# Attention with a GpSimd side job: another timetable for the side job, subtractions a slot earlier, one small transfer on another queue, two exponentials at another place

## The chip, the core and the metric

The program runs on one core of one Trainium2 chip. A core has TensorE (PE, matrix products into PSUM banks of 128 x 512 float32; its weight loads are shown apart as PEld), VectorE (DVE), ScalarE (ACT), GpSimd (POOL) and SyncE (SP). SP computes nothing here: it issues DMA transfers, and ACT can issue them too. Each engine works through its own list of instructions in order; an instruction that waits holds up all that stands behind it on that engine. The metric is the device time of one execution in microseconds (us).

## The reference

A transformer block of sequence length S = 2048 and width D = 448, cut to what matters here:

```python
h = layernorm(x) * (1 + ca) + sa                       # ca, sa, ... from silu(c) @ w_mod
q, k, v = split(h @ wqkv)                              # 16 heads of 28
p = softmax(q @ k.T * 28 ** -0.5)                      # 2048 x 2048 for each head
x = x + ga * ((p @ v) @ wo)
h = layernorm(x) * (1 + cb) + sb
z = gelu(h @ w_in)                                     # 2048 x 1792: z1, z2
g = w_sp @ layernorm(z2) + b_sp                        # w_sp is 2048 x 2048
x = x + gb * ((z1 * g) @ w_out)
```

The inputs make the softmax's scores large, so a row's maximum has to be taken away before the exponential. The product with `w_sp` is done late in the program by a scheme with fewer block products, which needs sums and differences of blocks of `w_sp`. These weight sums have nothing to do with attention, but they are made while attention runs, on POOL.

## The kernel before, in words

The attention stage takes about half of the time. Its 16 heads have 16 key tiles of 128 keys each; `u` = 16 x head + key tile numbers the 256 units, and `pair(u)` writes out the work of two units. A number of a slot in this text is a value of `u`: events hang on a slot and are written out when the loop comes to it. So all orders are fixed by the program's text, engine by engine; nothing is decided on the chip.

For each head, three kinds of 128 x 512 products are made on PE:

- `m_mm` (tile `mt`): queries against keys, laid out so that DVE can reduce along the keys to the row maxima (`pm`). They run 20 slots ahead (`LEAD`). At slot 16h - 4 `m_max` reduces these to one number for each query, `m_fin` turns them (a PE transpose to `mtp`, a DVE copy to `nt`), and a small DMA writes `nt` as two rows, a high and a low part, into rows 84 and 85 of the tile `qst` of that head. With those rows in the contraction, each later product already has the maximum subtracted.
- `s_mm` (tile `st_ps`): the transposed scores with the maximum subtracted; ACT takes the exponential (tile `P`).
- for heads 1 to 13, called `RAW`, the first 512 queries go another way. `r_mm` (tile `rt`) makes the raw scores 21 slots ahead, ACT copies them to one of 23 `raw` tiles (their names are rawA, rawB, rawC), and DVE keeps a running maximum `rmax` from them, which `r_turn` turns at slot 16h - 6. When rows 84 and 85 have landed, `r_neg` at slot 16h - 1 spreads the negative maxima over all partitions (a PE product, an ACT copy to `rneg`). Then POOL adds `rneg` to each raw tile (`r_sub`, 16 in a head), and ACT takes the exponential (`x_exp`).

`pv_mm` (tile `o_ps`) multiplies the four `P` tiles of a unit with V, two units behind. A pair is thus, on PE: two `rt`, 16 short products of `pv_mm`, and six `mt` and six `st_ps` in turn. Seven PSUM banks go round among `mt`, `st_ps`, `rt` and the turned tiles. A bank is free again once ACT or DVE has read it.

At slot 16h + 2 SP loads the keys and queries of head h + 2 (`load_head`, one small and six larger DMAs). `n_sum`, `n_recip`, `n_bcast`, `n_mul` (POOL) and `n_scatter` normalize the previous head over slots 16h + 2 to 16h + 9; their DMAs are SP's too.

POOL has seven tiles `ws_raw` for the weight sums. The string `W_SUMS` says what is done at which slot: `98:4=w14.2` loads a block into tile 4 at slot 98, `99:0=1-3` subtracts on POOL, `-1` negates, `98:p12.1=0` stores tile 0, and a load from `p...` fetches a stored sum again. A load and a store are DMAs of 256 KB on SP. A sum that writes a tile waits until the store of what stood there is through.

Of the kernel before, what the change touches and what calls it, by code (L numbers as in the profile page):

```python
# [57 lines left out]
    "41:5=w0.0,0=4-0 42:2=0+3,p7.0=0 43:3=p20.0 44:0=2+5,-0 45:5=p0.0,2=4+0,-2,p8.0=0 46:0=3-0,p10.0=2 "
    "48:2=p22.0,0=0+5 49:4=w14.1,5=w13.1,1=1-3,p12.0=0 50:3=w2.1 51:0=1-2 52:1=4+5,-1,p24.0=0 "
    "53:2=w15.1,0=3-4,p15.1=1 54:p14.1=0 55:4=w11.1,0=5-0 56:1=2+5,p16.1=0 57:6=w7.1,p6.1=1 58:1=1-4 "  # L60
    "59:2=5-1,p9.1=1 60:5=w5.1,0=6+0,p11.1=2 61:p18.1=0 62:2=w1.1 63:0=6+5 64:5=w6.1,4=w4.1,p22.1=0 "
    "65:3=w3.1,2=6+2,-2 66:0=w8.1,p20.1=2 67:5=5+4,-5 68:3=6-3,p25.1=5 69:6=w12.1,p0.1=3 72:3=w9.1,6=0-6 74:6=6-4 "
    "75:p2.1=6 76:6=3-6 77:1=6-1 78:p17.1=1 79:2=w10.1,6=4-1 80:3=1-3,p21.1=6 82:6=w2.1,3=3-2 83:4=4-3,p3.1=3 "
    "84:p5.1=4 85:3=4-6 86:5=6+5,p23.1=3 87:6=w11.1,3=5+4 88:p13.1=3 89:0=2+0 90:2=w0.1,0=6-0 91:p7.1=0 92:0=0+4 "
    "93:3=p20.1,0=0+2,-0 94:4=p0.1,2=6+0,-2,p8.1=0 95:p10.1=2 96:0=3-0 97:2=p22.1,0=0+4 "
    "98:4=w14.2,5=w13.2,p12.1=0 99:0=1-3 100:3=w2.2,0=0-2 101:1=4+5,-1,p24.1=0 102:p15.2=1 103:2=w15.2,0=3-4 "
    "104:4=w11.2,1=5-0,p14.2=0 105:p16.2=1 106:0=2+5 107:6=w7.2,2=0-4,p6.2=0 108:0=5-2,p9.2=2 109:5=w5.2,p11.2=0 "
# [22 lines left out]
def tile_adaln_mha_gmlp(ctx, tc, x, wqkv, wo, w_in, w_spT, b_sp, w_out, cT, w_mod, out):  # L90
# [683 lines left out]
    def m_fin(h):  # L774
# [5 lines left out]
        dve.tensor_copy(nt, tp[0 : 2 * NT, 0:128])  # L780
# [4 lines left out]

    turned = []

    def m_rows(eng, h, nt):
        eng.dma_start(qst[h % 3][84:86, :].bitcast(F32), nt[:, :])
# [1051 lines left out]
```

## Time and profile before

| | us |
|---|---|
| median of three runs | 1364.48 |
| lowest and highest of the three | 1364.22 and 1367.44 |
| the profiled execution, its own time | 1367.31 |
| its span, first to last instruction | 1365.5 |
| PE busy in it | 1351.7 |
| DVE, ACT, POOL busy in it | 1084.3, 907.9, 604.0 |

The span is what the views of the trace are measured in; the device time of the same execution is 1.8 us longer, for what lies around the instructions. PE is listed as busy nearly all of the time. That number alone does not say how much there is to win: matmuls overlap, and a matmul that waits a tenth of a microsecond leaves no gap in it. So for the attention stage the distance between the same instruction in two neighbouring pairs says more: a pair without disturbance takes 5.3 us, and the views below are read by how far a pair or a head is from that.

### The profile page before, as it was taken

The numbers are of one execution on the slowest core, as the hardware profiler recorded it, in microseconds if no ns is written. First come the engines' busy times: TensorE is split into PE (matmuls) and PEld (weight loads), VectorE is DVE, ScalarE is ACT, GpSimd is POOL, SyncE is SP. The second block draws the span as 40 slices with busy tenths as digits, with TensorE's granted clock in tenths as the row PEclk, the third lists the DMA queues.
The fourth block names the chain that finished last, engine by engine and source line by source line (L and its number), as shares of the span: only waits on it lengthen the run. The fifth ranks groups of instructions, "written<-read, shape, count | busy, mean of one in ns | idle before, by whom it ended". The sixth has DMA issues, their size and how long they took to land.

```text
span 1365.5 us, 20681 instructions
## 1 busy us (share of the span) xinstructions
PE 1351.7 (99%) x6945; PEld 938.8 (69%) x6945; DVE 1084.3 (79%) x1777; ACT 907.9 (66%) x1687; POOL 604.0 (44%) x521
## 2 busy tenths in 40 slices
PE   9999999999999999999999999999999999999998
PEld 8888555555554555455555554988898888888898
DVE  7798889999998899889998870762269798889682
ACT  6623789999998999889997779364234654444221
...
GB/s 292 137 179 177 202 64 119 126 150 145 90 126 129 143 112 126 139 141 94 136 104 109 93 82 37 203 124 128 77 2 84 131 101 108 116 105 178 270 156 82
DMA packets 92870, 174.68 MB, mean 128 GB/s; under 512 B 16536, under 2 KB 31770, under 8 KB 90218
## 3 DMA queue, kind: packets, MB, share of 16 engines
...
q14 instruction: 51, 0.42, 0.1%
HBM read 111.71 MB, written 56.82 MB: 123 GB/s over the span
## 4 chain that ended last, share of the span: by engine, by line
PE 89%; POOL 3%; DMA 2%; DVE 2%; ACT 2%; issue 1%; SPq 0%; ACTq 0%; DVEq 0%; POOLq 0%
PE acc L1617 19%; PE o_ps L859 15%; PE mt L750 13%; PE st_ps L795 12%; PE z_ps L1509 5%; PE z_ps L1341 5%; PE pq L415 4%; PE rt L795 3%; PE wo_ps L1206 3%; DMA ws_scr<-ws_raw 2%; PE y_ps L1696 2%; PE y_ps L1697 2%; PE pv L397 2%; PE y_ps L1695 2%; ACT P L840 1%
## 5 line engine op out<-in xcount | busy, mean ns | idle before, releaser
L756 DVE TENSOR_REDUCE pm<-mt 128x1 f32<-128x512 f32 x816 | 507.3, 682 | 21.2 <-PE mt L750 20.8
L840 ACT ACTIVATE P<-st_ps 128x512 f32<-128x512 f32 x816 | 422.8, 624 | 63.6 <-PE st_ps L795 58.5
L750 PE MATMUL mt<-kst,qst 128*128 128x512 f32 x816 | 332.2, 411 | 1.6 <-DVE rmax L811 0.7
L795 PE MATMUL st_ps<-qst,kst 128*128 128x512 f32 x816 | 299.0, 402 | 4.2 <-ACT P L840 4.2
L859 PE MATMUL o_ps<-P,V 128*32 128x512 f32 x2048 | 250.7, 601 | 1.8 <-ACT P L840 0.6
L750 PEld LDWEIGHTS mt<-kst,qst 128*128 128x128 f32 x816 | 153.2, 188 | 114.4 <-DVE rmax L811 33.2
L1617 PE MATMUL acc<-wsp_h,heapA 128*128 128x512 f32 x752 | 231.6, 389 | 0.0
L795 PEld LDWEIGHTS st_ps<-qst,kst 128*128 128x128 f32 x816 | 152.3, 188 | 57.2 <-ACT P L840 9.8
L967 POOL TENSOR_TENSOR ws_raw<-ws_raw 128x512 f32<-128x512 f32 x124 | 160.1, 1292 | 57.0 <-DMA ws_scr<-ws_raw 41.4
L830 POOL TENSOR_TENSOR rawA<-rawA,rneg 128x512 f32<-128x512 f32 x126 | 160.4, 1292 | 28.6 <-ACT rneg L827 28.6
L1617 PEld LDWEIGHTS acc<-wsp_h,heapA 128*128 128x128 f32 x752 | 141.2, 188 | 29.3
L811 DVE TENSOR_TENSOR rmax<-rt,rmax 128x512 f32<-128x512 f32 x182 | 124.9, 686 | 31.0 <-ACT rawA L801 12.2
L1397 ACT ACTIVATE wsp_h<-raw_sp 128x512 fp32r<-128x512 f32 x104 | 65.6, 632 | 126.1 <-PE acc L1617 113.7
L1617 PE MATMUL acc<-wsp_l,heapA 128*128 128x512 f32 x376 | 146.3, 389 | 0.0
L859 PEld LDWEIGHTS o_ps<-P,V 128*32 128x32 f32 x2048 | 56.0, 109 | 120.8 <-issue 99.0
L830 POOL TENSOR_TENSOR rawB<-rawB,rneg 128x512 f32<-128x512 f32 x64 | 81.9, 1295 | 23.2 <-ACT rneg L827 23.2
L143 DVE TENSOR_TENSOR wsp_l<-raw_sp,wsp_h 128x512 fp32r<-128x512 f32 x104 | 70.4, 686 | 16.6 <-ACT wsp_h L1397 16.4
L1617 PEld LDWEIGHTS acc<-wsp_l,heapA 128*128 128x128 f32 x376 | 70.6, 188 | 14.6
L840 ACT ACTIVATE P<-rawA 128x512 f32<-128x512 f32 x126 | 77.4, 681 | 3.6 <-POOL rawA L830 3.6
L801 ACT ACTIVATE rawA<-rt 128x512 f32<-128x512 f32 x126 | 72.5, 659 | 0.0
L795 PE MATMUL rt<-qst,kst 128*128 128x512 f32 x208 | 70.2, 417 | 0.0
L415 PE MATMUL pq<-heapD,heapD 128*128 128x512 f32 x196 | 61.8, 390 | 0.0
...
## 6 DMA issues: line engine op xcount, KB each, us to landing
...
```

The lines of the kernel that those rows point to most:

```text
L143: eng.tensor_tensor(out=dst, in0=a, in1=hi.bitcast(F32), op=ALU.subtract)
L415: pe.matmul(pq, wqk[:, b, m * 128 : (m + 1) * 128], hT[g][:, a, :], start=j == 0, stop=j == NST - 1)
L750: pe.matmul(mt, qst[h % 3][:, t * 128 : (t + 1) * 128], kst[h % 3][:, kb * 512 : (kb + 1) * 512], start=True, stop=True)
L756: dve.tensor_reduce(out=pms[h][:, t, kb : kb + 1], in_=mt, axis=AX.X, op=ALU.max)
L795: pe.matmul(st, kst[h % 3][:, kt * 128 : (kt + 1) * 128], qst[h % 3][:, qb * 512 : (qb + 1) * 512], start=True, stop=True)
L801: act.activation(raw_tile(u), st, AF.Copy)
L811: dve.tensor_tensor(out=rmax[0], in0=st, in1=raw_tile(u - 1) if u % NT == 1 else rmax[0], op=ALU.max)
L830: pool.tensor_tensor(out=raw_tile(u), in0=raw_tile(u), in1=rneg[0], op=ALU.add)
L840: act.activation(p, src, AF.Exp, scale=SCALE)
L859: pe.matmul(otile[h][32 * qb : 32 * qb + 32, :], V[:, kt, h, :], ptiles.pop((u, qb)), start=kt == 0, stop=kt == NT - 1)
L967: pool.tensor_tensor(out=ws_tile(op[0]), in0=ws_tile(op[2]), in1=ws_tile(op[4]), op=ALU.add if op[3] == "+" else ALU.subtract)
L1617: pe.matmul(a[j], z[:, c], w, start=start and k == 0, stop=st == 3 and k == 2, skip_group_check=not new or j == 3)
```

## The change

Five edits, all of them to the order of the work.

1. `W_SUMS` has the same loads, sums, negations and stores, at other slots. No sum now stands in the slot after a store whose tile it writes; the least distance is two slots. Loads are two slots or more ahead of their use, where before it was three.
2. `r_sub` of key tile k runs at slot 16h + k - 4 (from tile 6 on) in place of 16h + k - 3; the first six stand at slots 16h - 1, 16h and 16h + 1, two each.
3. The rows `nt` of the RAW heads are sent by SP at once behind the DVE copy. Before, ACT sent them after the third `st_ps` of the pair (`n_o` counts the two `rt` as well).
4. In the first pair of a RAW head `x_exp` comes right behind the two copies of `rt`, as in the other pairs. Before, the two came after the fourth and the sixth `st_ps`.
5. For heads 14 and 15 `m_fin` is an event of the next slot.

```diff
 W_SUMS = (
-    "2:0=w14.0,1=w13.0 3:3=w2.0 5:2=0+1,-2 6:4=w15.0,0=3-0,p15.0=2 7:5=w11.0,2=1-0,p14.0=0 8:p16.0=2 9:0=4+1 "
...
+    "2:0=w14.0,1=w13.0,3=w2.0,4=w15.0,5=w11.0,6=w7.0 4:2=0+1,-2,0=3-0 5:p15.0=2,p14.0=0,3=w4.0 7:2=1-0,0=4+1,4=0-5 "
...
@@ m_fin
-        if h in RAW:
-            turned.append((h, nt))
-        else:
-            m_rows(sp, h, nt)
-
-    turned = []
-
-    def m_rows(eng, h, nt):
-        eng.dma_start(qst[h % 3][84:86, :].bitcast(F32), nt[:, :])
+        sp.dma_start(qst[h % 3][84:86, :].bitcast(F32), nt[:, :])
@@ the events
-        at(max(h * NT + NT - LEAD, -2), m_fin, h, when=late)
+        at(max(h * NT + NT - LEAD, -2) + (h > RAW[-1]), m_fin, h, when=events if h > RAW[-1] else late)
     for h in RAW:
         at(h * NT - 6, r_turn, h, when=late)
         at(h * NT - 1, r_neg, h)
         for k in range(NT):
-            at(h * NT + (k // 2 - 1 if k < 4 else k - 3), r_sub, h * NT + k)
+            at(h * NT + (k // 2 - 1 if k < 6 else k - 4), r_sub, h * NT + k)
@@ pair
-        xat = [len(R_) + 4, len(R_) + 6] if u % NT == 0 else [len(R_)] * 2
+        xat = [len(R_)] * 2
@@ pair, after s_mm
-                if n_o >= 5 and turned:
-                    m_rows(act, *turned.pop())
```

How this moves instructions shows at three places. On PE and DVE next to nothing moves: the one difference is that the transpose `mtp` of head 14 stands one `mt` later, and its copy one `pm` later.

ACT, from the maxima's rows of head 4 to its second pair, before. `P<-rawB` is an `x_exp`, `P<-st_ps` the exponential of an `s_mm`, `rawB<-rt` the copy of an `r_mm`:

```order
L789 DMA qst_873<-nt 2x16x128
L840 ACTIVATE P<-st_ps 128x512 x3
L801 ACTIVATE rawB<-rt 128x512 x2
L840 ACTIVATE P<-rawB 128x512 x2
L827 ACTIVATE rneg<-st_ps 128x512
L840 ACTIVATE P<-st_ps 128x512 x6
L801 ACTIVATE rawB<-rt 128x512 x2
L840 ACTIVATE P<-st_ps 128x512 x4
L840 ACTIVATE P<-rawB 128x512
L840 ACTIVATE P<-st_ps 128x512 x2
L840 ACTIVATE P<-rawB 128x512
```

And now, from the same place on:

```order
L830 ACTIVATE P<-st_ps 128x512 x6
L791 ACTIVATE rawB<-rt 128x512 x2
L830 ACTIVATE P<-rawB 128x512 x2
L817 ACTIVATE rneg<-st_ps 128x512
L830 ACTIVATE P<-st_ps 128x512 x6
L791 ACTIVATE rawB<-rt 128x512 x2
L830 ACTIVATE P<-rawB 128x512 x2
L830 ACTIVATE P<-st_ps 128x512 x6
```

The DMA has gone from ACT's list, and the two `x_exp` of the head's first pair stand ahead of its six other exponentials.

POOL at the beginning of head 6, before: `rawA<-rawA,rneg` is an `r_sub`, the `ws_raw` rows are weight sums (TENSOR_SCALAR a negation):

```order
L967 TENSOR_TENSOR ws_raw<-ws_raw 128x512 x2
L962 TENSOR_SCALAR ws_raw<-ws_raw 128x512
L967 TENSOR_TENSOR ws_raw<-ws_raw 128x512
L962 TENSOR_SCALAR ws_raw<-ws_raw 128x512
L830 TENSOR_TENSOR rawA<-rawA,rneg 128x512 x4
L967 TENSOR_TENSOR ws_raw<-ws_raw 128x512
L830 TENSOR_TENSOR rawA<-rawA,rneg 128x512
L967 TENSOR_TENSOR ws_raw<-ws_raw 128x512
L830 TENSOR_TENSOR rawA<-rawA,rneg 128x512 x2
L967 TENSOR_TENSOR ws_raw<-ws_raw 128x512
L830 TENSOR_TENSOR rawA<-rawA,rneg 128x512
```

And now, for head 5 (the first six rows) and head 6 (from the row with x2 ahead of x5 on):

```order
L820 TENSOR_TENSOR rawA<-rawA,rneg 128x512 x3
L820 TENSOR_TENSOR rawB<-rawB,rneg 128x512 x3
L957 TENSOR_TENSOR ws_raw<-ws_raw 128x512 x2
L820 TENSOR_TENSOR rawB<-rawB,rneg 128x512 x3
L957 TENSOR_TENSOR ws_raw<-ws_raw 128x512 x2
L820 TENSOR_TENSOR rawB<-rawB,rneg 128x512
...
L820 TENSOR_TENSOR rawA<-rawA,rneg 128x512 x2
L957 TENSOR_TENSOR ws_raw<-ws_raw 128x512 x2
L820 TENSOR_TENSOR rawA<-rawA,rneg 128x512 x5
L957 TENSOR_TENSOR ws_raw<-ws_raw 128x512
L820 TENSOR_TENSOR rawA<-rawA,rneg 128x512
```

In head 6 before, the sum behind the seventh subtraction (slot 99) writes the tile that is stored at slot 98, right behind the loads of head 8. Now the first sum of head 6 that waits for a transfer from behind those loads comes after ten subtractions; in head 5 it comes after nine (slot 84, for a store of slot 82).

SP around the rows of head 6 as it is now; `heapD_90<-osb` is `n_scatter`, `rt<-osb` is `n_sum`, and the `qst_875<-qst_875` row begins `load_head`:

```order
L890 DMA heapD_90<-osb 16x512 x4
L890 DMA heapD_90<-osb 12x512 x4
L955 DMA ws_raw<-in_w_spT_dram 128x512
L779 DMA qst_871<-nt 2x16x128
L949 DMA ws_scr<-ws_raw 128x512
L955 DMA ws_raw<-in_w_spT_dram 128x512
L949 DMA ws_scr<-ws_raw 128x512
L955 DMA ws_raw<-ws_scr 128x512
L955 DMA ws_raw<-in_w_spT_dram 128x512
L865 DMA rt<-osb 128x1x16
L670 DMA qst_875<-qst_875 2x2048
```

Before, the row `qst<-nt` was not in this list for heads 1 to 13. Now SP stops at it until DVE has written `nt`, and everything below it in the list comes later than that.

More of the change, by code (lines that the diff above doesn't have):

```diff
@@ L58 @@
[L58 to L67, printed above, removed]
@@ L78 @@
-    "181:5=5-0,p3.3=0 182:p5.3=5 183:0=5-6 184:p23.3=0 185:0=6+4 186:4=w11.3,0=0+5 187:p13.3=0 188:0=2+1 "
-    "189:2=w0.3,0=4-0 190:1=0+5,p7.3=0 192:5=p20.3,0=1+2,-0 193:2=p0.3,1=4+0,-1,p8.3=0 194:p10.3=1 195:0=5-0 "
-    "196:4=p22.3,0=0+2 197:1=3-5,p12.3=0 199:0=1-4 200:p24.3=0 "
+    "2:0=w14.0,1=w13.0,3=w2.0,4=w15.0,5=w11.0,6=w7.0 4:2=0+1,-2,0=3-0 5:p15.0=2,p14.0=0,3=w4.0 7:2=1-0,0=4+1,4=0-5 "
+    "8:p16.0=2,p6.0=0,5=w5.0,p9.0=4 10:0=1-4,1=6+2 13:p11.0=0,2=w1.0,p18.0=1 15:0=6+5,1=6+2 16:5=w6.0,p22.0=0 "
@@ new lines @@
+    "18:-1,0=w8.0 19:2=5+3,p20.0=1 20:-2,5=w3.0 21:p25.0=2,1=w12.0 22:5=6-5 23:6=w9.0,1=0-1,p0.0=5,1=1-3 24:p2.0=1 "
+    "25:5=w10.0 26:1=6-1,1=1-4 27:4=3-1 28:6=1-6,0=5+0 29:p17.0=1,p21.0=4 31:4=6-5,3=3-4 "
+    "32:6=w2.0,p3.0=4,p5.0=3,5=w0.0 34:4=3-6 35:p23.0=4,2=6+2 36:2=2+3,6=w7.1 37:4=w11.0,p13.0=2 39:0=4-0,2=0+3 "
+    "40:p7.0=0,3=p20.0 42:0=2+5,-0 43:2=4+0,-2 44:1=1-3 45:5=p0.0,p8.0=0,p10.0=2,4=w14.1 47:0=3-0,2=p22.0,0=0+5 "
+    "48:5=w13.1,p12.0=0,3=w2.1 50:0=1-2 51:1=4+5,p24.0=0,2=w15.1 52:-1 53:0=3-4,p15.1=1 54:p14.1=0,4=w11.1,3=w3.1 "
@@ new lines @@
+    "55:1=2+5 56:0=5-0,p6.1=1 57:p16.1=0,3=6-3 58:1=1-4,p0.1=3 59:2=5-1 60:0=6+0 "
+    "61:p9.1=1,5=w5.1,p11.1=2,p18.1=0,4=w4.1,3=w9.1 63:2=w1.1,0=6+5 64:5=w6.1,p22.1=0 65:2=6+2 66:-2,0=w8.1,6=w12.1 "
+    "67:p20.1=2,5=5+4 68:-5 69:p25.1=5,6=0-6,2=w10.1 70:6=6-4 71:p2.1=6,0=2+0 73:6=3-6 74:1=6-1 75:6=4-1 "
+    "76:3=1-3,3=3-2 77:p17.1=1,p21.1=6,4=4-3,p3.1=3,2=w0.1 78:p5.1=4 79:6=w2.1 81:3=4-6,5=6+5 82:p23.1=3,6=w11.1 "
+    "84:3=5+4,0=6-0 85:p13.1=3,p7.1=0,5=w13.2 87:0=0+4,3=p20.1,0=0+2,-0 88:4=p0.1,p8.1=0 89:2=6+0 90:-2,6=w7.2 "
@@ new lines @@
+    "91:0=3-0 92:0=0+4 93:p10.1=2,4=w14.2,p12.1=0 95:2=p22.1,0=1-3,1=4+5 96:3=w2.2 98:0=0-2 99:-1,p24.1=0,2=w15.2 "
+    "100:p15.2=1 101:0=3-4 102:4=w11.2,1=5-0,p14.2=0,3=w3.2 103:p16.2=1 104:0=2+5,2=0-4 "
+    "105:p6.2=0,p9.2=2,4=w4.2,3=6-3 106:p0.2=3 107:0=5-2 109:5=w5.2,p11.2=0,3=w9.2 111:0=6+1 112:1=w1.2,p18.2=0 "
+    "114:0=6+5,1=6+1 115:5=w6.2,p22.2=0,-1,6=w8.2 116:p20.2=1 117:5=5+4,-5,0=w12.2 118:p25.2=5,1=w10.2 "
+    "119:0=6-0,0=0-4 120:p2.2=0 122:0=3-0,0=0-2 123:2=4-0 125:p17.2=0,p21.2=2 127:2=0-3,2=2-1 128:3=w2.2,p3.2=2 "
@@ new lines @@
+    "130:2=4-2 131:4=2-3,p5.2=2 132:3=3+5,p23.2=4 133:5=w11.2,3=3+2 134:1=1+6,p13.2=3,4=w0.2 135:1=5-1,6=w7.3 "
+    "136:p7.2=1,3=p20.2 138:1=1+2,1=1+4 139:-1 140:2=5+1,-2 141:4=p0.2,p8.2=1,p10.2=2,5=p22.2,0=0-3 "
+    "143:1=3-1,1=1+4,2=w14.3 144:p12.2=1,4=w13.3,3=w15.3 146:1=w2.3,0=0-5 147:p24.2=0,5=w11.3 149:0=2+4,-0 "
+    "150:2=1-2,p15.3=0 151:p14.3=2,1=w8.3 152:0=4-2 153:2=3+4,p16.3=0,3=2-5 154:p6.3=2,p9.3=3,5=w4.3 155:0=6+0 "
+    "156:2=4-3 157:4=w5.3,p11.3=2,p18.3=0 159:2=w1.3,0=6+4 160:4=w6.3,p22.3=0 161:2=6+2 162:-2,0=w3.3 "
@@ L81 @@
+    "163:p20.3=2,4=4+5 164:-4 165:p25.3=4,0=6-0,2=w10.3 166:6=w12.3,p0.3=0 168:0=w9.3,6=1-6,6=6-5 169:p2.3=6 "
+    "171:6=0-6,3=6-3,6=5-3 172:0=3-0,0=0-2 173:p17.3=3,p21.3=6,5=5-0,p3.3=0 174:p5.3=5 175:6=w2.3 177:0=5-6 "
+    "178:p23.3=0 180:0=6+4,0=0+5 181:4=w11.3,p13.3=0 183:0=2+1,0=4-0,1=0+5 184:2=w0.3,p7.3=0,5=p20.3 186:0=1+2,-0 "
+    "187:1=4+0 188:-1 189:2=p0.3,p8.3=0,p10.3=1,4=p22.3 191:0=5-0,0=0+2 192:p12.3=0 194:1=3-5 195:0=1-4 196:p24.3=0 "
 )
```

14 lines of the change are left out of this document (removed).

## The prediction

> **What bounds the kernel now.** I read the page first, then the busy time by stretches, then the waits by engine, then the timeline at the heads that stand out.
>
> ```profile
> span 1365.5 us, 20681 instructions
> PE 1351.7 (99%) x6945; PEld 938.8 (69%) x6945; DVE 1084.3 (79%) x1777; ACT 907.9 (66%) x1687; POOL 604.0 (44%) x521
> ```
>
> PE holds the end: it is busy in 99% of the span. The change moves one PE instruction by one place, so all it can win is time that PE loses by waiting in the attention stage. The next view has one attention head in each stretch (from the first `o_ps` of one head's first pair to that of the next). Its columns are the stretch, its length, the busy time of PE, PEld, DVE, ACT and POOL with their instructions, the granted clock, the DMA share and GB/s.
>
> ```profile
> 377.40:421.60 44.20, 44.06 (x247) 23.85 (x246) 41.27 (x72) 41.20 (x82) 38.15 (x31) 1.00 0.42 121
> 421.60:468.80 47.20, 45.24 (x247) 23.75 (x246) 41.36 (x72) 41.08 (x82) 35.56 (x29) 1.00 0.47 136
> 557.20:605.70 48.50, 45.94 (x247) 24.13 (x246) 41.44 (x72) 41.21 (x82) 39.27 (x33) 0.96 0.47 134
> 605.70:649.90 44.20, 44.06 (x247) 23.84 (x246) 41.22 (x72) 41.17 (x83) 33.11 (x27) 1.00 0.47 120
> ```
>
> An ordinary head takes 44.2 us. Head 6 takes 3.0 and head 9 takes 4.3 more. DVE and ACT are each busy for 41.2 of an ordinary head's 44.2, so they are only 3 us behind PE, which matters below. Who was waited for in the two long heads:
>
> ```profile
> ACT P L840 <- POOL rawA L830: 3.6, 2, 2.1
> ACT P L840 <- POOL rawB L830: 3.3, 1, 3.3
> PE st_ps L795 <- ACT P L840: 4.2, 3, 2.4
> ```
>
> (us in total, times, the longest.) Head 9 in the timeline, then three stretches around it; then head 6, from the end of its `rneg` on:
>
> ```profile
> 574.61 1.29 POOL L967 TENSOR_TENSOR ws_raw<-ws_raw 128x512 f32<-128x512 f32 x1 [6.02 <-DMA ws_scr<-ws_raw]
> 578.73 0.63 ACT L840 ACTIVATE P<-rawB 128x512 f32<-128x512 f32 x1 [3.27 <-POOL rawB L830]
> 579.90 0.50 PE L795 MATMUL st_ps<-qst,kst 128*128 128x512 f32 x1 [2.37 <-ACT P L840]
> 577.00:580.00 3.00, 0.64 (x4) 0.21 (x2) 1.44 (x3) 1.27 (x3) 3.00 (x4) 1.00 0.73 227
> 580.00:583.00 3.00, 3.00 (x10) 1.35 (x14) 1.58 (x3) 3.00 (x7) 3.00 (x3) 0.59 0.34 128
> 583.00:586.00 3.00, 3.00 (x23) 1.31 (x16) 0.86 (x2) 1.30 (x3) 3.00 (x3) 0.84 0.25 57
> 413.19 0.60 ACT L827 ACTIVATE rneg<-st_ps 128x512 f32<-128x512 f32 x1 [0.22 <-PE st_ps L823]
> 421.35 1.26 SPq L674 DMA_DIRECT2D kst<-qk_scr  x3
> 424.91 0.39 SPq L959 DMA_DIRECT2D ws_scr<-ws_raw  x1
> 434.00 1.29 POOL L967 TENSOR_TENSOR ws_raw<-ws_raw 128x512 f32<-128x512 f32 x1 [7.59 <-DMA ws_scr<-ws_raw]
> 436.57 0.63 ACT L840 ACTIVATE P<-rawA 128x512 f32<-128x512 f32 x1 [2.10 <-POOL rawA L830]
> ```
>
> The chain is the same in both: a weight sum on POOL waits for a store, the subtractions behind it are late, ACT stops at an `x_exp`, no bank is freed, PE stops. In head 6 the store was issued at 424.91 behind the loads of a head (from 421.35), and POOL went on at 434.00, 9.1 us after the issue. In head 9 the gap of 2.4 us is followed by 6 us with a granted clock of 0.59 and 0.84: 3.0 x 0.41 + 3.0 x 0.16 = 1.7 us of its 4.3. The Trainium skill ("TensorE: Matmul & The Clock Gate", Part 1) lets the clock fall only after an idle window of about 3.4 us; by it the stall would have cost 2.6 us and not 4.3. The trace does not agree here, since its gap was shorter, and the measured heads go into the sum.
>
> **The weight sums and the subtractions one slot earlier (edits 1 and 2).** They remove these stalls if no other wait of POOL is as long. The sum that waited in head 6 stood behind seven subtractions. ACT wanted the eighth tile (number 7) at 436.57 - 2.10 = 434.47, 20.7 us after `rneg` was through at 413.79; tile 9 is wanted a pair (5.3) later, at 26.0. Now the most exposed sums, those of slot 84 in head 5 and slot 180 in head 11, wait for a store issued right behind a head's loads too, but nine subtractions are ahead of them. The price of a POOL operation is on the page:
>
> ```profile
> L830 POOL TENSOR_TENSOR rawA<-rawA,rneg 128x512 f32<-128x512 f32 x126 | 160.4, 1292 | 28.6 <-ACT rneg L827 28.6
> ```
>
> 160.4 / 126 = 1.27 us. Nine subtractions and two sums end 14.0 us after `rneg`. If the store lands as late as in head 6 (434.00 - 413.79 = 20.2), POOL waits 6.2 us, then does two sums and the subtraction of tile 9: 20.2 + 3.8 = 24.0, 2 us before ACT wants it. So the wait stays and is covered. The same row has 28.6 us in which POOL stood idle ahead of these subtractions, all of it until `rneg`: POOL usually comes early to a head, and a lateness of some us is made good before the next. I take the whole excess: 3.0 + 4.3 = **7.3 us** (ends: 0, if the stalls move to other heads, and 7.3).
>
> **The first pair of a head (edit 4).** An undisturbed pair and the next, then head 4's first pair and its second; under them ACT and DVE in head 4's first pair.
>
> ```profile
> 388.44 1.92 PE L859 MATMUL o_ps<-P,V 128*32 128x512 f32 x16
> 393.72 1.92 PE L859 MATMUL o_ps<-P,V 128*32 128x512 f32 x16
> 327.70 1.92 PE L859 MATMUL o_ps<-P,V 128*32 128x512 f32 x16
> 333.27 2.25 PE L859 MATMUL o_ps<-P,V 128*32 128x512 f32 x16
> 328.20 1.16 ACT L801 ACTIVATE rawB<-rt 128x512 f32<-128x512 f32 x2
> 330.34 2.07 ACT L840 ACTIVATE P<-st_ps 128x512 f32<-128x512 f32 x4 [0.98 <-PE st_ps L795]
> 332.26 0.65 ACT L840 ACTIVATE P<-rawB 128x512 f32<-128x512 f32 x1
> 333.74 0.67 ACT L840 ACTIVATE P<-rawB 128x512 f32<-128x512 f32 x1
> 330.90 0.68 DVE L869 COPY osb<-o_ps 128x512 f32<-128x512 f32 x1
> ```
>
> An ordinary pair takes 393.72 - 388.44 = 5.28; this one 333.27 - 327.70 = 5.57, and the sixteen products of V after it 2.25 in place of 1.92, since the second `x_exp` ended at 334.41, after they had begun. That is 0.29 + 0.33 = 0.62 us a head. The two exponentials (0.65 + 0.67) now fill ACT's idle 0.98 behind the copies, so the six others begin some 0.3 later than 330.34 and, at 2.07 / 4 each, end 3.1 later at 333.7; the 0.33 goes. Of the 0.29 some stays, because DVE has the 0.68 of `osb` in this pair on top of its share, as it has the turning of the maxima in the next place below, where DVE then holds PE back. I take 0.35 a head for the 12 heads 2 to 13: **4.2 us** (ends: 0, if DVE takes all of it, and 12 x 0.62 = 7.4). The condition is that tiles 0 and 1 are subtracted by the end of the copies, 328.20 + 1.16 = 329.4; head 4's `rneg` (the ACT row in the next fence) is through at 325.45, and two operations take 2.5, so 1.4 us is over. Each head that POOL enters later than that gives some of the 0.35 back.
>
> **The maxima's rows on SP (edit 3).** Head 4's pair of `m_fin`:
>
> ```profile
> 316.39 1.92 PE L859 MATMUL o_ps<-P,V 128*32 128x512 f32 x16
> 322.22 1.92 PE L859 MATMUL o_ps<-P,V 128*32 128x512 f32 x16
> 320.26 0.65 ACTq L789 DMA_DIRECT2D qst<-nt  x1
> 319.58 0.37 PEld L795 LDWEIGHTS st_ps<-qst,kst 128*128 128x128 f32 x2 [0.32 <-DVE rmax L811]
> 320.36 0.19 PEld L795 LDWEIGHTS st_ps<-qst,kst 128*128 128x128 f32 x1 [0.24 <-DVE pm L756]
> 320.96 0.19 PEld L795 LDWEIGHTS st_ps<-qst,kst 128*128 128x128 f32 x1 [0.30 <-DVE pm L756]
> 319.44 0.27 DVE L780 COPY nt<-mtp 32x128 f32<-32x128 f32 x1
> 280.64 0.60 ACT L827 ACTIVATE rneg<-st_ps 128x512 f32<-128x512 f32 x1 [0.22 <-PE st_ps L823]
> 324.85 0.60 ACT L827 ACTIVATE rneg<-st_ps 128x512 f32<-128x512 f32 x1 [0.24 <-PE st_ps L823]
> 324.41 0.40 PE L823 MATMUL st_ps<-qst,ones 128*128 128x512 f32 x1
> 768.38 0.28 PE L777 MATMUL mtp<-ident,mxp 128*32 128x128 f32 x1 [0.70 <-DVE mxp L772]
> ```
>
> The pair takes 5.83, and ACT spends 0.65 of it on the DMA. It looks like a cost, but every one of the weight loads that waits there waits for DVE, none for ACT. So I take **0** for the freed 0.65 (ends: 0 and 13 x 0.5 = 6.5). What it could cost: `nt` is ready at 319.71 and PE needs the rows at 324.41, so 4.7 us are there for issue and transfer. ACT used them up from 320.26 on; SP can start 0.5 us earlier if it is free. In the new order the last SP transfer ahead of head 4's rows is a store of slot 58, for a sum that is about the 24th POOL operation of head 3: 24 x 1.27 = 30.5 us after head 3's `rneg` was through at 281.24, where `nt` came 38.5 after it. So SP should have been free for 8 us, which also covers one wait of POOL like the 6.2 above. SP then stands still until `nt` comes; what is queued behind it there are transfers of sums whose users come after the next `rneg`, and the `n_sum` of the head, six slots (16 us) later. The Trainium skill ("DMA: Bandwidth & Descriptors", "Issuing engines are not separate DMA queues" and "Queues, rings and completion order") speaks against the edit: all queues share the 16 DMA engines, another issuer saves only sequencer time, and each of SP and ACT has rings of its own, consumed in order. By that rule the rows now stand behind SP's transfers; its result is the last rival below.
>
> **Head 14's transpose (edit 5)** stands one `mt` later. PE waited 0.70 for DVE at 768.38; one `mt` (0.23 from start to start) now fills part of it: **0.2 us** (ends 0 and 0.7).
>
> **Sum.** 7.3 + 4.2 + 0 + 0.2 = 11.7 us. The profiled execution's own time is 1367.31 (span 1365.5 and 1.8 around it), 2.8 above the median 1364.48, near the highest run. Whether the 2.8 are stalls of this kind or something that stays I can't tell: 1367.3 - 11.7 = 1355.6 or 1364.5 - 11.7 = 1352.8. I take the middle, 1365.9 - 11.7 = **1354.2**, in round numbers 1354.
>
> **The rivals.**
>
> *DVE or another POOL wait keeps a third of it.* DVE's 41.2 us of 44.2 leave 3 us in a head, and it holds PE back already in the pair of `m_fin`. If it does so in the first pair too, the 4.2 are lost: 1365.9 - 7.5 = 1358.4. The same comes out if a sum of slot 84 or 180 waits 3 us longer than 20.2 and half of the 7.3 comes back: 1357.9. For it: loads are now two slots (5.3 us) ahead of their use in place of three. Against: 2 us of margin. Chance 0.22.
>
> *The stalls only move.* The loads of a head are still there, and the transfers behind them still take 9 us. If the stalls come back in other heads, 7.3 are lost: 1365.9 - 4.4 = 1361.5, which is no change. Chance 0.12.
>
> *The rows come late on SP: slower.* If the transfers ahead of them on SP hold the 16 KB as the head's loads held the store (9.1 us from issue to release), `r_neg` comes 9.1 - 4.7 = 4.4 us late, and PE stands still that long with all `st_ps` behind it. In six of 13 heads that is 26 us: 1354 + 26 = 1380. It decides for slower from four heads on (4 x 4.4 is over 11.7 + 4.1). Against it: a head's loads are ten slots (26 us) ahead of the rows. The ring order that the Trainium skill states is what it rests on; no run here shows the rows on SP behind a load. Chance 0.08.
>
> **How the numbers follow.** Forecast 0.58, then 0.22, 0.12 and 0.08. A measurement of this kernel can tell 0.3%, 4.1 us, from no change. The forecast and most of the first rival (0.19 of 0.22) are below 1360.4: faster 0.77. The rest of it and the second: same 0.15. Slower 0.08. The range goes from 1349 (all upper ends but the ACT one, 7.3 + 7.4 + 0.7 = 15.4, below the median) to 1361, where the stalls that move begin; about 0.2 is outside.
>
> **What would show it.** Right: no row with ACT `P` waiting for POOL raw tiles, every head near 43.8, the `o_ps` of a head's second pair back at 1.92, the pair of `m_fin` still at 5.8. Wrong: PE waiting at the product `st_ps<-qst,ones`, ACT waiting for POOL in a head's first pair, or a head over 46 us.

## The result, and the profile after

| | before | after |
|---|---|---|
| median of four runs, us | 1364.78 | 1352.99 |
| lowest and highest, us | 1364.22 and 1367.44 | 1352.54 and 1353.12 |
| the profiled execution, its own time | 1367.31 | 1353.00 |
| its span | 1365.5 | 1351.2 |

The ratio is 0.9909, with a 95% interval from 0.9892 to 0.9926. The change makes the kernel 11.8 us faster, and the times now lie within 0.6 us of each other where before they lay within 3.2.

The page of the kernel after, with its two rows for POOL (count, busy us and mean ns, then the idle time ahead of them and what ended it):

```profile
span 1351.2 us, 20695 instructions
PE 1344.5 (100%) x6945; PEld 939.2 (70%) x6945; DVE 1082.2 (80%) x1777; ACT 908.5 (67%) x1687; POOL 604.2 (45%) x521
L820 POOL TENSOR_TENSOR rawA<-rawA,rneg 128x512 f32<-128x512 f32 x126 | 160.3, 1292 | 43.9 <-ACT rneg L817 43.9
L957 POOL TENSOR_TENSOR ws_raw<-ws_raw 128x512 f32<-128x512 f32 x124 | 159.7, 1291 | 20.8 <-DMA ws_scr<-ws_raw 16.7
```

Busy times are as before: the same work was done. POOL's idle time has moved. Ahead of the subtractions in the rawA tiles it is 43.9 us, where it was 28.6, all of it until `rneg`; so POOL now comes earlier to a head. Ahead of the weight sums only 16.7 us of it are waits for a store; before they were 41.4.

The view by stretches, for heads 4, 6 and 9 of the kernel after (columns as in the prediction; each stretch begins one pair earlier than there, at the products of V in a head's first pair, and is one head long as before):

```profile
325.61:369.42 43.81, 43.81 (x247) 23.97 (x247) 41.08 (x73) 41.20 (x82) 39.28 (x32) 1.00 0.47 130
413.23:457.04 43.81, 43.81 (x247) 23.96 (x246) 41.10 (x72) 41.20 (x82) 34.16 (x28) 1.00 0.47 135
544.66:588.46 43.80, 43.80 (x248) 23.96 (x247) 41.08 (x73) 41.23 (x82) 35.41 (x29) 1.00 0.53 144
```

Heads 6 and 9, which took 47.2 and 48.5, now take what head 4 takes. An ordinary head took 44.2 and takes 43.8. In the waits by engine no row of ACT's exponentials (`P`) waiting for POOL is left. Waits of POOL for a store are still up to 5.2 us long. Here is the one of head 5, on which the prediction had put a margin, with POOL's next subtraction and the two exponentials of ACT that need it:

```profile
POOL ws_raw L957 <- DMA ws_scr<-ws_raw: 16.7, 7, 5.2
385.30 2.53 POOL L957 TENSOR_TENSOR ws_raw<-ws_raw 128x512 f32<-128x512 f32 x2 [4.29 <-DMA ws_scr<-ws_raw]
387.78 1.30 POOL L820 TENSOR_TENSOR rawB<-rawB,rneg 128x512 f32<-128x512 f32 x1
392.07 1.21 ACT L830 ACTIVATE P<-rawB 128x512 f32<-128x512 f32 x2
```

POOL waited 4.29 us, and tile 9 was still through at 389.08. ACT came for tiles 8 and 9 at 392.07. The longest wait, 5.16 us in head 11 (slot 180), was covered in the same way: tile 9 was through 3.3 us before ACT came for tiles 8 and 9.

The first pair of head 4, in the timeline:

```profile
325.61 1.92 PE L849 MATMUL o_ps<-P,V 128*32 128x512 f32 x16
331.17 1.92 PE L849 MATMUL o_ps<-P,V 128*32 128x512 f32 x16
326.10 1.16 ACT L791 ACTIVATE rawB<-rt 128x512 f32<-128x512 f32 x2
327.05 1.23 ACT L830 ACTIVATE P<-rawB 128x512 f32<-128x512 f32 x2
328.23 3.08 ACT L830 ACTIVATE P<-st_ps 128x512 f32<-128x512 f32 x6
328.80 0.68 DVE L859 COPY osb<-o_ps 128x512 f32<-128x512 f32 x1
329.89 0.19 PEld L785 LDWEIGHTS st_ps<-qst,kst 128*128 128x128 f32 x1 [0.29 <-ACT P L830]
330.73 0.19 PEld L785 LDWEIGHTS rt<-qst,kst 128*128 128x128 f32 x1 [0.17 <-DVE pm L754]
```

The two `x_exp` fill ACT right behind the copies, and the products of V of the next pair take 1.92 in place of 2.25. The pair itself is as long as before, 331.17 - 325.61 = 5.56: PE waits 0.29 for an exponential of ACT in it and 0.17 for DVE at its end; before, the same two waits were 0.24 and 0.19. So what a head gained came all from the second pair.

The pair of `m_fin` of head 4:

```profile
314.29 1.92 PE L849 MATMUL o_ps<-P,V 128*32 128x512 f32 x16
317.48 0.37 PEld L785 LDWEIGHTS st_ps<-qst,kst 128*128 128x128 f32 x2 [0.32 <-DVE rmax L801]
317.63 0.69 SPq L779 DMA_DIRECT2D qst<-nt  x1
318.26 0.19 PEld L785 LDWEIGHTS st_ps<-qst,kst 128*128 128x128 f32 x1 [0.24 <-DVE pm L754]
320.12 1.92 PE L849 MATMUL o_ps<-P,V 128*32 128x512 f32 x16
```

It takes 5.83, to the hundredth what it took before, and PE waits for DVE in it as before, though ACT has lost 0.65 us of work there. Where edit 3 did help, the experiments show.

### The profile page after: what moved, and what is told of

It is laid out like the page before. It is cut to its first block, busy times and chain, and to the rows that moved or that the text cites. A ratio compares the mean times of both kernels' runs of the same rounds, so it can differ in the third digit from the quotient of the medians.

```text
span 1351.2 us, 20695 instructions
## 1 busy us (share of the span) xinstructions
PE 1344.5 (100%) x6945; PEld 939.2 (70%) x6945; DVE 1082.2 (80%) x1777; ACT 908.5 (67%) x1687; POOL 604.2 (45%) x521
## 4 chain that ended last, share of the span: by engine, by line
PE 97%; DVE 2%; ACT 0%; issue 0%; POOL 0%; DVEq 0%; ACTq 0%
PE acc L1605 19%; PE o_ps L849 17%; PE mt L748 15%; PE st_ps L785 14%; PE z_ps L1497 5%; PE z_ps L1329 5%; PE pq L413 4%; PE rt L785 4%; PE wo_ps L1194 3%; PE y_ps L1685 2%; PE y_ps L1683 2%; PE pv L395 2%; PE y_ps L1684 2%; DVE pm L754 1%; PE rtp L806 1%; PE tp L191 1%
## 5 line engine op out<-in xcount | busy, mean ns | idle before, releaser
L849 PE MATMUL o_ps<-P,V 128*32 128x512 f32 x2048 | 247.3, 598 | 0.0
L820 POOL TENSOR_TENSOR rawA<-rawA,rneg 128x512 f32<-128x512 f32 x126 | 160.3, 1292 | 43.9 <-ACT rneg L817 43.9
L957 POOL TENSOR_TENSOR ws_raw<-ws_raw 128x512 f32<-128x512 f32 x124 | 159.7, 1291 | 20.8 <-DMA ws_scr<-ws_raw 16.7
```

Of the source, the lines that this page charges most:

```text
L820: pool.tensor_tensor(out=raw_tile(u), in0=raw_tile(u), in1=rneg[0], op=ALU.add)
L849: pe.matmul(otile[h][32 * qb : 32 * qb + 32, :], V[:, kt, h, :], ptiles.pop((u, qb)), start=kt == 0, stop=kt == NT - 1)
L957: pool.tensor_tensor(out=ws_tile(op[0]), in0=ws_tile(op[2]), in1=ws_tile(op[4]), op=ALU.add if op[3] == "+" else ALU.subtract)
```

## The experiments

Each edit alone, then the change with one edit undone, then the two places where PE still waits. All times are medians. The runs were made on several chips, each beside runs of the kernel before on the same chip, whose medians are 1364.1 to 1366.6. So a small difference between runs of two chips is to be read with care.

### Edit 1 alone: the new table

```diff
-W_SUMS = ( ...the slots of before... )
+W_SUMS = ( ...the slots of the change... )
```

> The kernel before with the new timetable of the weight sums alone (edit 1). Theory: the stalls of heads 6 and 9 came from a sum that stood one slot behind a store issued after a head's loads; the new table has no such sum, so both heads are near 44.2 us and the time falls by about 7 (1357 to 1359); ACT has no wait for POOL over 1 us. Rival: the earlier subtractions are what covers the wait, and without them the stalls turn up at slots 84 and 180 (heads 5 and 11) with 2 to 4 us each: 1361 to 1365.

Measured: 1359.74 us (1359.38 to 1360.84), ratio 0.9960 (0.9947 to 0.9973), 4.7 us less than the 1364.45 beside it. Heads 6 and 9 in its view by stretches, and its row in the waits by engine:

```profile
415.26:459.42 44.16, 44.02 (x248) 23.87 (x247) 41.18 (x73) 41.16 (x83) 34.12 (x28) 1.00 0.46 134
547.75:591.98 44.23, 44.04 (x248) 23.84 (x247) 41.20 (x73) 41.23 (x83) 35.36 (x29) 1.00 0.52 145
POOL ws_raw L965 <- DMA ws_scr<-ws_raw: 22.2, 8, 5.9
```

Both long heads are ordinary, and no exponential of ACT waits for POOL. Against the profiled execution of before (1367.31) this is 7.6 us, against the median 4.7. The five runs spread over 1.5 us, the twenty of before beside them over 5.1 (1362.56 to 1367.64).

### Edit 2 alone: the subtractions a slot earlier

```diff
-            at(h * NT + (k // 2 - 1 if k < 4 else k - 3), r_sub, h * NT + k)
+            at(h * NT + (k // 2 - 1 if k < 6 else k - 4), r_sub, h * NT + k)
```

> The kernel before with the subtractions four tiles ahead alone (edit 2). By the count, the waiting sum of head 6 has eight subtractions ahead of it in place of seven; POOL goes on 20.2 us after rneg, does two sums and tile 8 by 24.0, and ACT wants tile 8 at 25.3. Theory: this edit alone removes the stalls as well, 1357 to 1360, with POOL's waits for stores unchanged (over 35 us in total). Rival: the old table's waits are too long or too many in a row (head 9), and at least half of the 7.3 us stays: 1361 to 1365.

Measured: 1360.06 us (1359.92 to 1361.53), ratio 0.9963 (0.9950 to 0.9976). Head 6 in the same view, the waits, and a row of DVE in head 7:

```profile
416.11:460.27 44.16, 44.04 (x247) 23.86 (x246) 41.22 (x73) 41.27 (x82) 34.80 (x28) 1.00 0.50 143
POOL ws_raw L967 <- DMA ws_scr<-ws_raw: 43.2, 19, 6.0
473.79 0.25 DVE L879 RECIPROCAL rt<-rt 128x16 f32<-128x16 f32 x1 [1.23 <-DMA rt<-osb]
```

POOL waits for stores as long as before (43.2 us beside 41.4), but no exponential of ACT waits for POOL. (This execution is the highest of the five. Its head 7 has a pair of 6.64 in place of 5.3: DVE stood 1.23 us until the transfer of `n_sum` had landed, the last row, with the readers of PE's banks behind it. So this is another stall, not one of POOL.) So edits 1 and 2 are two cures for one ailment: the one takes POOL's waits away, the other lets them happen and covers them.

### The change without edit 2, and without edit 1

```diff
-            at(h * NT + (k // 2 - 1 if k < 6 else k - 4), r_sub, h * NT + k)
+            at(h * NT + (k // 2 - 1 if k < 4 else k - 3), r_sub, h * NT + k)
```

> The changed kernel with edit 2 undone: subtractions three tiles ahead. By the count, the sum of slot 84 has eight subtractions ahead of it; POOL goes on 20.2 us after rneg at the latest and has tile 8 ready by 24.0, ACT wants it at 25.3. Theory: with the new timetable the fourth tile of lead is not needed, 1352.5 to 1354. Rival: the lead is needed, since the exponentials of a head now start earlier, and one or two heads stall by 1 to 3 us: 1355 to 1358.

Measured: 1353.14 us (1352.33 to 1353.42), the time of the whole change. With the new table, the slot of lead is worth nothing that can be measured: one exponential of ACT waits 0.7 us for POOL without it, and no head is longer.

```diff
-W_SUMS = ( ...the slots of the change... )
+W_SUMS = ( ...the slots of before... )
```

> The changed kernel with edit 1 undone: the old timetable of the weight sums. Theory: the lead of four tiles covers most of the waits, but POOL enters heads 6, 7 and 9 late by 1 to 3 us and the early first exponentials then wait for it, and SP has stores open when the maxima's rows come: 1355 to 1360, with a spread over 2 us from run to run. Rival: the lead alone is enough, 1352.5 to 1354. Rival the other way: the rows behind stores on SP make r_neg wait in several heads, over 1362.

Measured: 1358.39 us (1358.13 to 1359.16): 5.4 more than the whole change, though edit 2 is in it. What is lost here is not ACT waiting for POOL, which comes to 1.1 us in all. SP and PE at the rows of head 4, in the timeline, and three stretches around it:

```profile
312.59 5.28 SPq L951 DMA_DIRECT2D ws_scr<-ws_raw  x2
320.04 0.33 SPq L957 DMA_DIRECT2D ws_raw<-in_w_spT_dram  x1
320.42 0.42 SPq L951 DMA_DIRECT2D ws_scr<-ws_raw  x1
320.94 0.69 SPq L781 DMA_DIRECT2D qst<-nt  x1
324.01 0.47 PE L815 MATMUL st_ps<-qst,ones 128*128 128x512 f32 x1 [2.01 <-DMA qst<-nt]
321.00:324.00 3.00, 1.00 (x9) 0.21 (x2) 1.62 (x3) 0.69 (x2) 0.26 (x1) 1.00 0.77 259
324.00:327.00 3.00, 2.99 (x9) 2.38 (x10) 1.38 (x2) 2.23 (x5) 1.81 (x2) 0.63 0.29 95
327.00:330.00 3.00, 3.00 (x19) 1.70 (x21) 2.49 (x4) 2.66 (x6) 3.00 (x3) 0.81 0.02 3
```

`nt` was written by 317.13, but SP stood at transfers of late weight sums and issued the rows at 320.94, 3.8 us later. PE stood 2.01 us at the product `st_ps<-qst,ones`, and then ran 6 us at a granted clock of 0.63 and 0.81. Head 3, to which this pair belongs, took 47.6. This is the prediction's "rows late on SP" at work, in the first of two places; the other cost 1.5 us in head 6. So edit 3 needs edit 1: the new table is what keeps SP free when `nt` comes.

### Edit 3 alone: the rows on SP, old table

```diff
-        if h in RAW:
-            turned.append((h, nt))
-        else:
-            m_rows(sp, h, nt)
+        m_rows(sp, h, nt)
```

> The kernel before with the maxima's rows of heads 1 to 13 on SP alone (edit 3). Theory: heads 2 to 13 do not change, their pair of m_fin stays at 5.83 us since DVE holds it; head 1's pair, where ACT has eight exponentials and three copies, gains about 0.8 us: 1363 to 1365. Rival: with the old table SP is still busy with a store when the rows are ready, r_neg's product waits for them, 1 to 4 us in several heads: 1368 to 1385.

Measured: 1365.31 us (1362.58 to 1372.72, eleven runs), ratio 1.0008 (0.9994 to 1.0022): no difference that can be told, and the widest spread of all. Head 3 and the waits of POOL in its profiled execution:

```profile
282.17:326.90 44.73, 44.26 (x247) 23.85 (x246) 41.19 (x73) 41.10 (x82) 35.44 (x29) 1.00 0.48 138
POOL ws_raw L964 <- DMA ws_scr<-ws_raw: 60.0, 17, 17.1
```

Head 3 is 0.5 us longer than the 44.2 of before, while head 0's pair of the rows (units 12 and 13) is 0.8 shorter. The wait of 17.1 us is in head 0: a sum on POOL waits for a store that stands on SP behind the rows, and goes on at 188.22, 3.2 us after `nt` was written (185.04). The longest wait before was 7.6. This execution is the lowest of the eleven; where the higher ones lose their time was not seen. By the medians, what the rows gain in head 0 is given back elsewhere. The record has the mean granted clock of each execution: 1.000 in the eight lowest, 0.997 and 0.996 in the two highest (1369.88 and 1372.72). By estimate (0.003 and 0.004 of the time) that is 4.1 and 5.5 us of clock in these two, as behind the long gaps of PE in the traces above; no trace shows where their gaps lie.

### The change without edit 3

```diff
-        sp.dma_start(qst[h % 3][84:86, :].bitcast(F32), nt[:, :])
+        if h in RAW:
+            turned.append((h, nt))
+        else:
+            m_rows(sp, h, nt)
...
+                if n_o >= 5 and turned:
+                    m_rows(act, *turned.pop())
```

> The changed kernel with edit 3 undone: the maxima's rows of heads 1 to 13 on ACT again, behind the third exponential. Theory: only head 1's pair at slot 12, the one with more ACT work than PE work, needs it off ACT, and this run is about 0.8 us slower than the changed kernel (1353 to 1354.5); the m_fin pairs of heads 2 to 13 stay at 5.83. Rival: ACT's 0.65 counts in every head now that the first exponentials stand earlier, 13 x 0.4: 1357 to 1359.

Measured: 1354.99 us (1354.24 to 1355.57), 2.0 more than the whole change. Most of it lies in two pairs. (In the profiled execution, 2.6 above that of the change, the first pair of head 8 has 0.35 more, 5.91 in place of 5.56; why was not tried.) First head 0, ACT and PE in the timeline:

```profile
185.24 1.26 ACTq L787 DMA_DIRECT2D qst<-nt  x1
187.26 0.50 PE L748 MATMUL mt<-kst,qst 128*128 128x512 f32 x1 [0.67 <-ACT P L838]
```

The issue of the rows took ACT 1.26 us here, where the median of the thirteen is 0.65, and PE waited 0.67 for the exponential behind it. The pair takes 7.12; in the whole change 6.32. Then the rows of head 4, ACT, SP and PE:

```profile
317.67 0.34 SPq L963 DMA_DIRECT2D ws_raw<-in_w_spT_dram  x1
318.07 1.17 SPq L957 DMA_DIRECT2D ws_scr<-ws_raw  x2
318.87 0.65 ACTq L787 DMA_DIRECT2D qst<-nt  x1
323.97 0.47 PE L821 MATMUL st_ps<-qst,ones 128*128 128x512 f32 x1 [0.81 <-DVE pm L754]
```

ACT sent them 0.57 after `nt` was written, among three transfers of 256 KB that SP issued from 317.67 to 319.24 (two began ahead of it, the third 0.05 after), and the product came 5.10 us after the issue. In ten of the other twelve heads it came 4.1 after the issue without a wait. The profile puts the 0.81 of idle time down to a `pm`, which came last by its semaphores. The semaphore of the transfer itself is in the trace too: the rows had landed at 323.83, 4.96 us after the issue and 0.14 before the product, where in the other twelve heads they landed 2.2 to 3.7 us after it. In the old-table run above, where the profile names the transfer, both products also began 0.14 after its semaphore. So the rows held the product. With the rows on SP, issued 0.02 after `nt` and so ahead of these transfers, the product comes 4.70 after `nt` as in most other heads, and the pair takes 5.49 in place of 6.55.

The Trainium skill ("DMA: Bandwidth & Descriptors", "Issuing engines are not separate DMA queues") lets another issuer save sequencer time alone. That is what the 0.8 us of head 0 are; the 1.06 of head 3 come from when the rows were issued beside SP's own transfers, which the move changed too.

### Edit 4 alone: the first exponentials

```diff
-        xat = [len(R_) + 4, len(R_) + 6] if u % NT == 0 else [len(R_)] * 2
+        xat = [len(R_)] * 2
```

> The kernel before with a head's first two exponentials at the front alone (edit 4). Theory: 0.33 us for each of 12 heads, 4 us: 1360 to 1361; the products of V in a head's second pair take 1.92 us again, and the first pair stays near 5.55. Heads 6, 7 and 9, which POOL enters 1.3 to 2.9 us late in the old table, give 0 to 2 us each back by ACT waiting for tiles 0 and 1, which would make it 1361 to 1364. Rival: DVE's copy takes the place of the wait and nothing is won: 1364 to 1365.

Measured: 1362.27 us (1361.22 to 1363.92), ratio 0.9981 (0.9972 to 0.9991), 2.2 less than before. The products of V in the second pair are at 1.92 and ordinary heads at 43.8, as in the whole change: some 0.4 for each of 12 heads would be 4.8. What is missing shows in the waits, and in the first pair of head 6:

```profile
ACT P L840 <- POOL rawA L830: 4.3, 4, 2.0
413.87 5.03 POOL L830 TENSOR_TENSOR rawA<-rawA,rneg 128x512 f32<-128x512 f32 x4
416.44 0.63 ACT L840 ACTIVATE P<-rawA 128x512 f32<-128x512 f32 x1 [0.41 <-POOL rawA L830]
```

With the old table POOL comes late to heads 6 and 7, and ACT, which now wants tiles 0 and 1 at once, waits for them with six exponentials behind it. The two first pairs took 5.86 and 6.04 in place of 5.55. Heads 6, 7 and 9 of this execution are 3.2, 0.4 and 2.2 above 43.8: 5.8 us of stalls, where edit 1 took 4.7 away from the median of before. So the price of edit 4 depends on POOL being early, which edit 1 sees to: with edits 1, 2, 4 and 5 together (the run before this one) the time is 1354.99, 4.75 below edit 1 alone.

Edit 4 moves one thing more than the list of changes says. The program's text keeps a `clock`, an estimate of when ACT and DVE will be done with what they have (`clock.read` and `clock.spend` are no instructions), and gives each product the PSUM bank that is free first by it. So another order of the exponentials also puts some products, most of them in a head's second pair, into other banks. Edits 1, 2 and 3 leave the banks as they were. The 0.33 of edit 4 is read from the products of V, which no longer wait for the second `x_exp`; no run has edit 4 with the banks of before.

### The 0.27 us left in a head's first pair

The first pair takes 5.55 where an ordinary one takes 5.28. DVE has the copy `osb` (0.68) there. First, the copy on ACT:

```diff
-            clock.spend("dve", 0.6)
-            dve.tensor_copy(osb[h], otile.pop(h))
-        else:
-            act.activation(osb[h], otile.pop(h), AF.Copy)
+            clock.spend("act", 0.477)
+        act.activation(osb[h], otile.pop(h), AF.Copy)
```

> The changed kernel with the copy of o_ps to osb of each head (n_copy, 0.68 us) on ACT in place of DVE. If DVE's copy is what keeps a head's first pair at 5.55, and ACT has room for it, the pair falls to 5.30 and the time by 13 x 0.25 = 3.2 us to about 1350. If ACT has no room (copies 1.16, two exponentials 1.32, six 3.1 and now 0.65 make 6.2 of work in a pair of 5.3), ACT becomes the one that holds the pair, at 5.6 to 6.1: 1354 to 1360. If neither engine holds it, nothing changes.

Measured: 1352.81 us (1352.57 to 1354.16), the same as the whole change; the first pair stays at 5.55. In its timeline ACT is busy without a gap from the copies to the end of the pair, and PE's second `rt` waits at the same place as before:

```profile
331.00 0.19 PEld L785 LDWEIGHTS rt<-qst,kst 128*128 128x128 f32 x1 [0.25 <-DVE pm L754]
```

The row names DVE even now that DVE has 0.68 less to do. The wait of 0.29 for ACT is gone, although ACT's six exponentials begin later, 2.95 us after the pair's start in place of 2.62. Here the banks moved too, since the edit changes a `clock.spend`: in the whole change the product that waits 0.29 gets a bank that another `st_ps` had only five products before, and with the copy on ACT it gets one that has been left for seven. So this run does not separate DVE's load from the choice of banks, and the next two don't either. Next, half of the copy for each:

```diff
-            clock.spend("dve", 0.6)
-            dve.tensor_copy(osb[h], otile.pop(h))
+            clock.spend("dve", 0.35)
+            clock.spend("act", 0.3)
+            o = otile.pop(h)
+            dve.tensor_copy(osb[h][:, 0:256], o[:, 0:256])
+            act.activation(osb[h][:, 256:512], o[:, 256:512], AF.Copy)
```

> The changed kernel, with the copy of `osb` in a head's first pair split: DVE copies columns 0 to 255, ACT columns 256 to 511 (in the kernel all 512 on DVE, with the copy on ACT alone the first pair stayed at 5.55). Theory (DVE and ACT are both so full in this pair that either of them, given the whole 0.68, holds PE back by the same 0.27): each has half of it now, the first pair falls from 5.55 to about 5.4 and the time by 13 x 0.15 = 2.0, to 1351.0. Rival (the 0.27 is not the copy's but comes with the bank that PE has to change at the end of a head): first pair 5.55, time 1353.0.

Measured: 1365.49 us (1365.13 to 1366.22), 12.5 more than the whole change. Neither theory had this. The timeline of head 4's first pair:

```profile
331.29 0.41 DVE L861 COPY osb<-o_ps 128x256 f32<-128x256 f32 x1
331.79 0.38 ACT L862 ACTIVATE osb<-o_ps 128x256 f32<-128x256 f32 x1 [1.02 <-PE st_ps L785]
332.71 0.49 PE L785 MATMUL st_ps<-qst,kst 128*128 128x512 f32 x1 [0.65 <-ACT P L830]
```

ACT's half begins 0.09 after DVE's half has ended. In the program it waits for it: both halves read one tile and write one tile, and the one written second in the program has a wait for the first one's semaphore. DVE's half stands behind two `pm`, so ACT idles 1.02 with six exponentials behind it, and the pair takes 6.51. The releaser that the profile names, a product of PE, is not the one that held it. The run says what a wait across two engines costs here (0.96 x 13 = 12.5 us), and nothing on the halves. So the halves once more, ACT's first in the program, together with the `nt` of the next section:

```diff
...
+            act.activation(osb[h][:, 256:512], o[:, 256:512], AF.Copy)
+            dve.tensor_copy(osb[h][:, 0:256], o[:, 0:256])
...
```

> The changed kernel with `nt` copied by ACT (1351.5 when that was done alone) and the copy of `osb` split again, this time with ACT's half ahead in the program. In the run where DVE's half stood first, the ACT half waited for it: in head 4 ACT stood idle 1.02 us behind the second `x_exp` and began 0.09 after DVE's half had ended, with six exponentials behind it, and the first pair took 6.51. Theory (it was that wait alone; both engines have room for a half each): ACT's half starts right behind the second `x_exp`, the first pair falls from 5.54 to about 5.4, and the time by 13 x 0.14 = 1.8 to 1349.7. Rival (a half on ACT ahead of the six exponentials is enough to hold PE back as the whole copy did): first pair 5.55, 1351.5.

Measured: 1350.72 us (1350.33 to 1351.15), ratio 0.9888 (0.9872 to 0.9905), the fastest of all runs. ACT's half starts right behind the second `x_exp`, and the first pair takes 5.51 in place of 5.55. That is 0.04 a head and not the 0.14 of the theory. So the 0.27 does not follow the copy from engine to engine in proportion, and taking the copy off DVE does not remove it. What holds PE there stays open. DVE's load alone fits badly: in the whole change DVE itself idles 0.52 us in this pair, waiting for ACT's first copy of `rt`. Two things were not tried: the banks held fixed, and the copy `rneg` (0.60), which ACT has in the pair before. ACT's first copy begins 0.49 after the start of a head's first pair, and 0.24 to 0.28 after that of most ordinary pairs.

### The pair of `m_fin`: who holds it

```diff
-        clock.read("dve", 0.3)
-        dve.tensor_copy(nt, tp[0 : 2 * NT, 0:128])
+        clock.read("act", 0.3)
+        act.activation(nt, tp[0 : 2 * NT, 0:128], AF.Copy)
```

> The changed kernel, with the copy `nt` of the turned maxima (32 x 128, 0.27 on DVE) made by ACT. Theory (DVE, with the four small reductions and this copy, sets the 5.83 of the pair of `m_fin`): the pair falls to about 5.6, and the time by up to 13 x 0.25 = 3.2, to about 1350. Rival (the 5.83 is set by the four reductions and the wait for the turn ahead of it, before the copy comes): pair 5.83, time 1353; and if ACT's place for the copy lies behind three exponentials, the rows come late and the product of `rneg` waits: over 1353.

Measured: 1351.50 us (1351.10 to 1351.62), ratio 0.9901 (0.9888 to 0.9915), 1.5 below the whole change. Head 4's pair in the timeline:

```profile
313.91 1.92 PE L849 MATMUL o_ps<-P,V 128*32 128x512 f32 x16
316.09 0.26 ACT L778 ACTIVATE nt<-mtp 32x128 f32<-32x128 f32 x1
319.55 1.92 PE L849 MATMUL o_ps<-P,V 128*32 128x512 f32 x16
```

The pair takes 5.64 in place of 5.83. Taking 0.65 off ACT (edit 3) did nothing to it; taking 0.27 off DVE shortened it by 0.19. With PE's waits in this pair, which all name DVE, that speaks for DVE as the one that holds it: its six `pm` behind the copy begin 3.05 us after the pair's start in place of 3.25. It is not a clean proof, because the edit also frees the bank of `mtp` 0.9 us earlier and puts some products of this pair and the next into other banks. 0.19 in 11 heads (1 to 11) would be 2.1; the time shows 1.5.

The split of the first try (DVE's half first) and this edit together:

> Both of these: split copy of `osb`, and `nt` on ACT. If the two are independent, the sum of their gains below 1353.0 (theory: 5.2, 1347.8). If ACT, at 41.2 us of a head's 43.8, has no room for both, less than the sum.

Measured: 1363.86 us (1363.23 to 1364.35), 1.6 below the 1365.49 of the spoiled halves, about what the copy of `nt` gives alone (1.5). So the gain of the one place does not depend on the other; the sum of the theory, 1347.8, could not come with halves that cost 12.5.

## Why the prediction was right or wrong

The predicted 1354 stands beside 1353.0, which is 1.0 less, and the direction and the mechanism hold. By the chain of runs, edit 1 gave 4.7 (1364.45 to 1359.74), edits 2, 4 and 5 on top of it 4.75 (to 1354.99), and edit 3 then 2.0 (to 1352.99). These steps join runs of different chips; measured against the kernel before on its own chip, each (1364.45, 1364.12 and 1364.78), they are 4.7, 4.4 and 2.7. The terms do not stand as they were written, and that the total came within 1 us is in part luck: the stalls were priced too high, the rows on SP at nothing, and the two errors nearly cancel.

**Weight sums and subtractions, 7.3.** The mechanism is as told: late sum, late subtractions, ACT, PE. The size failed: 7.3 was read from the one profiled execution, which the text itself placed near the highest run, and between medians it is 4.7. The open question there, whether the 2.8 us above the median were stalls of this kind, gets a likely answer from the spreads: 3.2 us before, and 0.6 with the stalls gone. The granted clock on record fits: of the 21 executions of before beside the split copy, the eight highest (from 1365.24 on) all have a mean of 0.999, and of the thirteen lower ones eleven have 1.000, so the high ones seem to hold a gap of PE after which the clock fell, as the profiled one does. Only that one has a trace. Taking the middle as the base gave back half of the difference, 1.4 of 2.6. What the step also missed is that edits 1 and 2 are each enough alone; it priced them as one, and nothing in it would have told that the second adds nothing.

**The covered wait.** A sum of slot 84 was to be released 20.2 us after `rneg` and tile 9 to be through at 24.0, 2 us early. It was released at 385.30 - 367.15 = 18.15 and the tile through at 21.9, 3.0 us before ACT came. The wait stays and is covered, as written.

**The first pair, 0.35 x 12 = 4.2.** Measured 0.4 a head (44.2 to 43.8; head 1, which the 12 leave out, gained 0.3 as well), and the split was right: the 0.33 behind the pair went, the 0.29 of the pair stayed. The reason given for the part that stays, DVE's copy of `osb`, was not borne out: moved to ACT, the pair stayed at 5.55, and split it fell by 0.04. Since these runs changed the banks too, DVE is not ruled out either; the step stays open. The condition on POOL was right: where POOL came late (edit 4 alone, heads 6 and 7) the gain went into waiting.

**The rows on SP, 0.** The argument that DVE holds the pair of `m_fin` held as far as it was tried, and the pair did not move. The term was still mis-sized; it measured 2.0 to 2.7, inside the stated ends of 0 and 6.5. The step looked at head 4's pair alone and took it for all thirteen. Head 0's was to be seen before, in the timeline of the kernel before:

```profile
185.49 1.27 ACTq L789 DMA_DIRECT2D qst<-nt  x1
187.51 0.50 PE L750 MATMUL mt<-kst,qst 128*128 128x512 f32 x1 [0.67 <-ACT P L840]
```

There the issue takes 1.27, not 0.65, and PE does wait for ACT behind it: worth 0.8. The other 1.06, rows beside SP's burst in head 3, is not in the kernel before (5.48). It is not in edit 1 alone either, where the same pair takes 5.51 with the new table and the rows on ACT. So it could be read neither from the trace nor from the new order alone: it hangs on when the transfers fall.

**The transpose of head 14, 0.2.** The pair went from 6.43 to 5.91, so 0.5, within the ends of 0 and 0.7. No run has this edit alone, but the pair takes 6.43 or 6.44 in all four kernels of edits 1 to 4 alone. PE's wait ahead of `mtp` fell from 0.70 to 0.24.

**The rivals.** "DVE or another POOL wait keeps a third": 0.27 do stay in the first pair, whether DVE keeps them is open, and they were not in the forecast's gain; no POOL wait came back. "The stalls only move": they did not; every head from 2 to 11 is within 0.2 of 43.8. "The rows come late on SP": it did not happen in this change, but it is a real mechanism. With the old table the change is 5.4 us slower than with the new, most of it in two heads (3.8 and 1.7 above 43.8), not 26 in six. It comes not because the transfer takes 9 us, but because SP itself stands at a transfer that waits for a sum, 3.8 us past `nt`. The reason given against it (SP free for 8 us in the new order) is what edit 1 provides, though with less in hand: in the trace of the change SP's last transfer ahead of head 4's rows was issued by 312.84, and `nt` came 4.8 us later.

**The clock.** The sentence on the Trainium skill ("TensorE: Matmul & The Clock Gate", Part 1, an idle window of about 3.4 us) has a second row against it: after the gap of 2.01 us in the old-table run the clock was 0.63 and 0.81 for 6 us.
